# First rows of w_out loaded in halves of columns, five "lower" steps on GpSimd, two products begun ahead of the first transposes

## The chip, the cores and the metric

The kernel runs on one core of a Trainium2 chip. The metric is the device time of one execution in microseconds (us); smaller is better. All inputs are float64 in device memory, so every weight arrives as pairs of 32-bit words and is turned into float32 on the chip.

## What is computed

Causal attention with 12 heads (2 batches, sequence 448, head size 64), then two feed-forward layers on its 896 x 768 output:

```python
scores = scale * q @ k.T                     # causal mask, softmax
x = softmax(scores) @ v                      # 896 x 768
h = ((x @ w1) * (x @ w2)) @ w3 @ w_out       # w1, w2: 768 x 1024, w3: 1024 x 1024, w_out: 1024 x 768
y = relu(h @ w_in2) ** 2 @ w_out2            # w_in2: 768 x 2048, w_out2: 2048 x 768
```

w3 and w_out stand behind each other with nothing between them, so the kernel multiplies w3 @ w_out first, while attention runs, and applies the product W (1024 x 768) later.

## The kernel before, in words

**Attention.** It goes through 12 pairs of heads. A pair p has these steps on TensorE: the scores (`scores`, L611, 16 matmuls, called S below), the transposes of the two heads' probabilities (`transposes`, L684, 20 transposes, T), and the product with v (`attend`, L705, 16 matmuls, A). Between S and T, VectorE takes the masked minimum out of PSUM (L653), ScalarE does the exponential (L663), VectorE takes reciprocals of the sums (L671, L672) and scales the blocks (L680). Between T and A, ScalarE copies the transposes out of PSUM (L701). S and T share six PSUM banks in turn: T of pair 0 reuses those of S of pair 1, so the minimum of pair 1 has to be done before T of pair 0 can end.

**W.** A unit `w_half(g, i, n)` (L549) makes one block of 128 rows by 384 columns (column half n) of W from one row block of w3 and four row blocks of w_out, with g for the two halves of the inner sum; there are 32 units. The first two row blocks of w3 (`PLAIN`, L146) are multiplied in float32 as they are (8 matmuls); the others are split into high and low parts and take 12 matmuls. `w_row` (L506) prepares a whole row block: `load_raw` (L460) issues its load on SP's queue, `float32` (L473) turns the words into float32 in three steps: prelu on ScalarE from the high words (L478), lower on VectorE from the low words, in place (L482), and join on VectorE of both (L486). Where a row is to be split, a cast on ScalarE (L432) and a subtraction on VectorE (L425) follow. Raw rows lie in three buffers taken in turn, and two rows of w_out (`LENT`, L149) in buffers lent by another pool; the second row of w3 comes into the buffer of the first, and so its load waits for the join of the first.

**Order.** The order on TensorE is that in which the steps are added: S0, S1, a filler of 36 transposes of a constant (`warm`, L746), T0, A0, S2, and from there on units of W between the steps (`fill`, L758, and the loop at L762). All other engines get their order from the planner `Program.order` (L59): a step's due time comes from TensorE's order, counted back through the prices given with each step, and at each moment an engine takes the ready step with the earliest due time. A wait written into an engine's queue holds what stands behind it. The weight loads keep their own order among each other (`turn="loads"`, L480).

After attention come w1, w2, W, w_in2 and w_out2, as one stream of matmuls (`bank`).

Of the kernel before, what the change touches and what calls it, by code (L numbers as in the profile page):

```python
# [8 lines left out]
F32 = mybir.dt.float32  # L9
F32R = mybir.dt.float32r  # L10
U32 = mybir.dt.uint32
AF = mybir.ActivationFunctionType
ALU = mybir.AluOpType
# [111 lines left out]
def attention_moe_moe2(ctx: ExitStack, tc: tile.TileContext, qk, v, w1, w2, w3, w_out, w_in2, w_out2, out):  # L125
# [18 lines left out]
    SLOTS8 = 8  # L144
    RAW = 3
    PLAIN = 2  # L146
    WARM = 36
    CLOSE = 4
    LENT = (("wout", 2), ("wout", 3))  # L149
    PAUSE = 64  # L150
# [23 lines left out]
    source = {"wout": w_out, "w1": w1, "w2": w2, "w3": w3, "win2": w_in2, "wout2": w_out2}  # L174
    raws, hls = {}, {}

    def load(key, pool, tag):
        src = source[key[0]][key[1]]
        n = src.shape[-1]
        t = pool.tile([P, DM, 2], U32, tag=tag, name=f"raw_{key[0]}_{key[1]}")  # L180
        nc.sync.dma_start(out=t[:, :n].rearrange("p f w -> p (f w)"), in_=src.bitcast(U32))
        raws[key] = t[:, :n]

    def halves(x):
        return x.rearrange("p (n c) -> p n c", c=HN)
# [147 lines left out]

    prog = Program({"S": 700})
    pools = {}
    engine_of = {"A": nc.scalar, "V": nc.vector}

    def act(width, psum=False, strided=False):
        gap = 60 + 0.815 * width if psum else 75 + (0.96 if strided else 0.845) * width
        return {"A": (gap, gap + 105)}  # L340

    def dve(width, fast=False):
        gap = 70 + (0.52 if fast else 1.038) * width
        return {"V": (gap, gap + 85)}
# [110 lines left out]
    def turn(what, n):  # L455

        count[what] += 1
        return (count[what] - 1) % n

    def load_raw(key):  # L460

        if key in LENT:
            pool, tag, place = ringb, "ringb", ("ringb", turn("lent", 4))
        elif key in order and turn("plain", RAW) == RAW - 1:
            pool, tag, place = rawb, "rawb", ("rawb", 0)
        else:
            pool, tag, place = rawp, "raw", ("raw", turn("raw", 2))
        words = [place + (s,) for s in "hl"]
        size = source[key[0]][key[1]].shape[-1] / DM
        prog.add({"S": (2200 * size, 2500 + 2200 * size)}, lambda e: load(key, pool, tag), [], words, turn="loads")  # L470
        return words

    def float32(key, words, width, y, names):  # L473

        high, low = words

        def prelu(e):
            nc.scalar.activation(y(), raws[key][:, :, 1].bitcast(F32), AF.Prelu, scale=2.0 ** -112, alpha=-2.0 ** 32)  # L478

        def lower(e):  # L480
            x = raws[key][:, :, 0]
            nc.vector.tensor_scalar(x, x, 2.0 ** -29, 7.0, ALU.mult, ALU.min)  # L482

        def join(e):
            yi = y().bitcast(U32)
            nc.vector.scalar_tensor_tensor(  # L486
                yi, yi, 3, raws.pop(key)[:, :, 0], op0=ALU.logical_shift_left, op1=ALU.bitwise_or)

        prog.add(act(width, strided=True), prelu, [high], names)
        prog.add(dve(width, fast=True), lower, [low], [low])  # L490
        prog.add(dve(width), join, [low, *names], names)

# [11 lines left out]
    def w_row(key):  # L506

        if key in w_rows:
            return
        kind, n = key  # L510
        words = load_raw(key)
        if kind == "w3":
            names = [("w3", n % 2, s) for s in "hl"]
            if n < PLAIN:
                w_rows[key] = names[:1]
                float32(key, words, W3N, lambda: w3_tile(n)[:, 0].bitcast(F32), names[:1])
                return
            hi, lo, width = lambda: w3_tile(n)[:, 0], lambda: w3_tile(n)[:, 1], W3N
        elif n < NB:
            names = [("ring", i, s) for i in (2 * n, 2 * n + 1) for s in "hl"]  # L520
            hi, lo, width = lambda: ring_pair(2 * n)[0], lambda: ring_pair(2 * n)[1], DM
        else:
            place = turn("lent", 4)
            names = [("ringb", place, s) for s in "hl"]
            hi, lo, width = lambda: ringb_tile(n)[:, 0], lambda: hls["wout", n][:, 1], DM
        row = 2 + n if kind == "wout" and n < NB else turn("f32", 2)
        x = lambda: xs[:, row, :width]
        src = [("xs", row, i) for i in range(2)]
        float32(key, words, width, x, src)
        y = x if kind == "w3" else lambda: halves(x())  # L530
        his, los = [m for m in names if m[2] == "h"], [m for m in names if m[2] == "l"]
        prog.add(act(width), copy(hi, y), src, his)
        prog.add(dve(width), tt(lo, y, lambda: hi_of(key).bitcast(F32), ALU.subtract), src + his, los)
        w_rows[key] = names

    def hi_of(key):
        kind, n = key
# [11 lines left out]
    def w_half(g, i, n):  # L549
        n3, cols = g * KF + i, slice(n * HN, (n + 1) * HN)  # L550
        plain = n3 < PLAIN
        for key in order[:order.index(("w3", n3)) + 1] + [("wout", g * NB + f) for f in range(NB)]:
            w_row(key)
        place, acc = turn("w", 2), []
        reads = list(w_rows["w3", n3])
        for f in range(NB):
            reads += [("xs", 2 + f, j) for j in range(2)] if plain else w_rows["wout", g * NB + f]

        def run(e):
            acc.append(ps_w.tile([P, HN], F32, tag="w", name=f"w{n3}_{n}"))  # L560
            for f in range(NB):
                c = slice(f * P, (f + 1) * P)
                if plain:
                    mm(acc[0], w3t[n3][:, 0, c].bitcast(F32), xs[:, 2 + f, cols], f == 0, f == NB - 1)
                    continue
                t, wo = w_parts(("w3", n3)), w_parts(("wout", g * NB + f))
                for s, r in ((0, 0), (0, 1), (1, 0)):
                    mm(acc[0], t[s][:, c], wo[r][:, n],
                       f == 0 and (s, r) == (0, 0), f == NB - 1 and (s, r) == (1, 0))

        t0 = (3.72 if plain else 3) * NB * HN * PE_ROW + 100
        prog.add({"T": (t0, t0 + 170)}, run, reads, [("w", place)])
        dst = wraw[i][:, cols]
        if g == 0:
            prog.add(dve(HN) | act(HN, True), copy(lambda: dst, lambda: acc[0]), [("w", place)], [("wraw", i, n)])
            return
        if n == 0:
            add = negated(lambda: dst, lambda: acc[0], lambda: dst, ALU.subtract)
        else:
            add = tt(lambda: dst, lambda: acc[0], lambda: dst, ALU.add)  # L580
        prog.add(dve(HN), add, [("w", place), ("wraw", i, n)], [("wraw", i, n)])
        if n == 1:
            prog.add({"S": (1200, 3000)}, lambda e: nc.sync.dma_start(out=w_dram[i // 2, i % 2], in_=wraw[i]),
                     [("wraw", i, 0), ("wraw", i, 1)], [("wdram", i)])
# [120 lines left out]
    def attend(p):  # L705
        place = turn("w", 2)

        def run(e):
            vt = v_t[p]
            x = x_t[p] = ps_w.tile([P, S], F32, tag="w", name=f"x{p}")  # L710
            for c in range(NCH):
                for j in range(2):
                    mm(x[j * D:(j + 1) * D, c * CP:], vt[:, c, j],
                       pt_t[2 * p + j][:, coff[c]:coff[c] + S - c * CP], c == 0, c == NCH - 1)

        pts = [("pt", h % 3, i) for h in (2 * p, 2 * p + 1) for i in range(len(PT))]
        prog.add({"T": (2038, 2270)}, run, pts + [("v", p % 2)], [("w", place)])
        return place
# [27 lines left out]
    def warm():  # L746
        place = turn("w", 2)

        def run(e):
            t = ps_w.tile([P, HN], F32, tag="w", name="warm")  # L750
            for _ in range(WARM):
                nc.tensor.transpose(t[:CP, :CP], ident[:CP, :CP], ident[:CP, :CP])

        prog.add({"T": (WARM * 96, WARM * 96 + 160)}, run, [], [("w", place)])

    w_units = [(g, i, n) for g in range(N3 // KF) for i in range(KF) for n in range(2)]

    def fill(n=1):  # L758
        for _ in range(n):
            w_half(*w_units.pop(0))  # L760

    for p in range(NP_ALL + 1):  # L762
        if p < NP_ALL:
            load_pair(p)
            load_v(p)
            scores(p)
            for j in range(2):
                softmax(p, j)
        if p == 1:
            warm()  # L770
        if p > 0:
            fill(p > 1)
            transposes(2 * p - 2)
            transposes(2 * p - 1)
            fill(1 if p == NP_ALL else 2 if p >= CLOSE else p > 1)
            place = attend(p - 1)
            x_parts(p - 1, place)
            fill(1 < p < CLOSE)
    assert not w_units

    def end_attention(e):
# [577 lines left out]
```

## Time and profile before

| what | value |
|---|---|
| median of 3 runs | 525.2 us (523.92 to 526.38) |
| the profiled execution's own time | 524.11 us |
| its span | 522.3 us |
| TensorE busy | 511.7 us, 98% of the span |
| VectorE busy | 484.6 us, 93% |
| ScalarE busy | 397.7 us, 76% |
| GpSimd busy | 15.0 us, 3% |

How to read it: the rows further down come from one profiled execution. Times count from the start of the span. PE is TensorE, PEld its weight loads, DVE VectorE, ACT ScalarE, POOL GpSimd, SP the queue that issues most transfers. "L172" is a line of the kernel; where a helper issues all matmuls, the tile's name tells them apart (s: scores, pp: transposes, x: product with v, w: units of W, bank: everything after attention). Brackets behind a row of the timeline hold the idle time ahead of it and what ended it. Float32 matmuls show as two instructions each, so a unit of four float32 products has eight.

### The profile page before, as it was taken

How to read it: one execution, taken by the hardware profiler on the slowest of the kernel's cores; microseconds unless marked ns; L12 is line 12 of the kernel's file. 1: busy time of each engine (PE TensorE's matmuls, PEld its weight loads, DVE VectorE, ACT ScalarE, POOL GpSimd, SP SyncE). 2: the span in 40 equal slices, each digit the busy share in tenths (PEclk: the TensorE clock that was granted, in tenths of full speed). 3: DMA queues.
4: the chain of work that ended last, by engine and by line, in shares of the span. 5: the costliest groups of instructions: out<-in, count | busy, mean ns of one | idle time of the engine just before them, and what ended most of it. 6: DMA issues, size and time to landing. Idle time of an engine off the chain costs nothing.

```text
span 522.3 us, 8468 instructions
## 1 busy us (share of the span) xinstructions
PE 511.7 (98%) x2905; PEld 461.3 (88%) x2905; DVE 484.6 (93%) x1140; ACT 397.7 (76%) x925; POOL 15.0 (3%) x20
## 2 busy tenths in 40 slices
PE   6899999999999999999999999999999999999996
PEld 5658888888889999999999999999999999999996
DVE  5999998889999999988875899999999999999996
ACT  5989988767869574637566568997999689969971
POOL 1000000000000010222100000000000000000000
PEclk9999999999999999999999999999999999999999
DMA  8957455452651459999672311504440355045114
GB/s 318 320 184 227 175 177 169 133 176 63 249 179 65 181 184 248 242 267 259 123 217 95 122 60 44 198 2 148 172 164 1 130 178 177 1 129 184 52 60 152
DMA packets 26571, 81.29 MB, mean 156 GB/s; under 512 B 2400, under 2 KB 13408, under 8 KB 26528
## 3 DMA queue, kind: packets, MB, share of 16 engines
q1 hardware_dynamic: 22752, 75.24, 42.5%
q0 software_dynamic: 3776, 5.51, 6.6%
q8 instruction: 23, 0.38, 0.3%
q14 instruction: 20, 0.16, 0.1%
HBM read 74.84 MB, written 14.55 MB: 171 GB/s over the span
## 4 chain that ended last, share of the span: by engine, by line
PE 94%; ACT 2%; DVE 2%; DMA 1%; issue 0%; DVEq 0%
PE bank L172 69%; PE w L172 13%; PE x L172 4%; PE s L172 4%; PE pp L695 4%; ACT p L663 1%; ACT xs L478 1%; DMA qk<-in_qk 1%; DVE p L653 0%; DVE p L680 0%; ACT pt L701 0%; DVE xs L486 0%; DVE g L425 0%; DVE w L486 0%; ACT w L478 0%; DVE st L672 0%
## 5 line engine op out<-in xcount | busy, mean ns | idle before, releaser
L432 ACT CAST ring<-xs 128x384 fp32r<-128x384 f32 (+1 forms) x194 | 102.7, 545 | 39.7 <-PE bank L172 21.9
L172 PE MATMUL bank<-xT,ring 128*128 128x448 f32 x630 | 132.0, 366 | 0.0
L172 PEld LDWEIGHTS bank<-xT,ring 128*128 128x128 f32 x630 | 117.9, 188 | 9.1
L425 DVE TENSOR_TENSOR ring<-xs,ring 128x384 fp32r<-128x384 f32 (+1 forms) x194 | 111.3, 588 | 13.1 <-ACT ring L432 12.5
L172 PE MATMUL bank<-ring,g 128*128 128x384 f32 x600 | 104.8, 334 | 0.0
L172 PEld LDWEIGHTS bank<-ring,g 128*128 128x128 f32 x600 | 104.1, 188 | 0.2
L172 PE MATMUL bank<-xB,ring 128*128 128x448 f32 x489 | 102.2, 366 | 0.0
L172 PEld LDWEIGHTS bank<-xB,ring 128*128 128x128 f32 x489 | 91.7, 188 | 7.4
L663 ACT ACTIVATE p<-p,st 112x224 f32<-112x224 f32 (+3 forms) x96 | 50.1, 534 | 10.0 <-DVE st L653 10.0
L425 DVE TENSOR_TENSOR xs<-xs 128x384 f32<-128x384 f32 x96 | 51.7, 551 | 0.2
L653 DVE CUSTOM_DVE_ANT_0 p<-s,mask 112x224 f32<-112x224 f32 (+3 forms) x96 | 36.6, 443 | 5.9 <-PE s L172 5.9
L432 ACT CAST g<-fs 128x384 fp32r<-128x384 f32 (+1 forms) x88 | 35.3, 414 | 7.8 <-DVE fs L425 7.7
L425 DVE TENSOR_TENSOR g<-fs,g 128x384 fp32r<-128x384 f32 (+1 forms) x88 | 36.6, 431 | 0.2
L172 PE MATMUL w<-hl_wout,w 128*128 128x384 f32 x192 | 36.2, 340 | 0.0
L432 ACT COPY fs<-bank 128x448 f32<-128x448 f32 (+1 forms) x52 | 27.5, 529 | 8.9 <-PE bank L172 8.7
L172 PEld LDWEIGHTS w<-hl_wout,w 128*128 128x128 f32 x192 | 32.9, 188 | 1.3 <-DVE fs L425 0.9
L172 PE MATMUL s<-qk 64*112 64x112 f32 (+3 forms) x192 | 27.4, 425 | 4.3 <-DMA qk<-in_qk 4.3
L478 ACT ACTIVATE xs<-raw_w 128x768 f32<-128x768 f32 (+1 forms) x30 | 24.2, 812 | 7.0 <-DVE w L425 3.2
L172 PE MATMUL bank<-ab,ring 128*128 128x448 f32 x144 | 29.5, 365 | 0.0
L680 DVE TENSOR_SCALAR p<-p,st 112x448 f32<-112x448 f32 (+1 forms) x96 | 29.1, 360 | 0.1
L172 PEld LDWEIGHTS bank<-ab,ring 128*128 128x128 f32 x144 | 27.1, 188 | 2.1
L172 PEld LDWEIGHTS s<-qk 64*112 64x112 f32 x192 | 15.4, 181 | 14.3 <-issue 6.0
(80 smaller groups left out, 687.2 us busy)
## 6 DMA issues: line engine op xcount, KB each, us to landing
raw_wout<-in_w_out SPq DMA_DIRECT2D x24, 768.0 KB, 4.5
raw_w<-in_w SPq DMA_DIRECT2D x16, 768.0 KB, 4.8
raw_win<-in_w_in SPq DMA_DIRECT2D x16, 768.0 KB, 4.2
raw_w<-in_w SPq DMA_DIRECT2D x16, 512.0 KB, 4.6
qk<-in_qk SPq DMA_DIRECT2D x12, 448.0 KB, 5.3
s_dram<-w_dram POOLq DMA_DIRECT2D x8, 576.0 KB, 9.5
w_dram<-wraw SPq DMA_DIRECT2D x8, 384.0 KB, 2.7
s_dram<-w_dram SPq DMA_DIRECT2D x4, 768.0 KB, 6.9
```

What stands on the lines that cost most here:

```text
L172: return nc.tensor.matmul(o, l, r, start=start, stop=stop, **more)
L425: return lambda e: engine_of[e].tensor_tensor(out(), x(), y(), op=what)
L432: return lambda e: engine_of[e].copy(out(), x()) if e == "A" else engine_of[e].tensor_copy(out(), x())
L478: nc.scalar.activation(y(), raws[key][:, :, 1].bitcast(F32), AF.Prelu, scale=2.0 ** -112, alpha=-2.0 ** 32)
L653: prog.add({"V": (gap, gap + 160)}, lambda e: nc.vector.tensor_tensor_reduce(block(p, j, i), s_t[p, j, g][:CP, o:o + w], mask[:, S - w:], ...
L663: prog.add({"A": (gap, gap + 100)}, lambda e, i=i: nc.scalar.activation(block(p, j, i), block(p, j, i), AF.Exp, bias=st_t[p][:, 0, j, i:i ...
L680: lambda e, i=i: nc.vector.tensor_scalar(block(p, j, i), block(p, j, i), st_t[p][:, 3, j, i:i + 1], None, ALU.mult),
L695: nc.tensor.transpose(x[0][:CP, o * CP:(o + 1) * CP], block(p, j, i)[:, c * CP:(c + 1) * CP], ident[:CP, :CP])
```

## The change

Three things are done.

- The first four row blocks of w_out are loaded and turned into float32 in two halves of 384 columns each, with a step of its own for each half (`w_columns`). A float32 unit of column half n asks for the four halves n only, and for its row of w3.
- The lower step of these eight halves and of the first row of w3 runs on GpSimd (engine "P" of the planner, priced at 100 + 1.3 ns for each column).
- The order on TensorE is written out as a list (`ORDER`; K is the filler, W the next unit). One unit stands between the filler and T0, one between T0 and A0, one each between S2 and T1 and between T1 and A1, and so on; the first four units go by column half: both rows with half 0, then both with half 1. The filler has 20 transposes instead of 36.

```diff
-    WARM = 36
+    WARM = 20
...
-    def load(key, pool, tag):
+    def load(key, pool, tag, cols=None):
         src = source[key[0]][key[1]]
         n = src.shape[-1]
...
+        x, src = raws[key], src.bitcast(U32)
+        if cols is not None:
+            x, src = x[:, cols], src[:, 2 * cols.start:2 * cols.stop]
+        nc.sync.dma_start(out=x.rearrange("p f w -> p (f w)"), in_=src)
...
+    GB, GS = 100, 1.3
+    POOLED = (("w3", 0), *(("wout", f) for f in range(4)))
...
         def lower(e):
-            x = raws[key][:, :, 0]
-            nc.vector.tensor_scalar(x, x, 2.0 ** -29, 7.0, ALU.mult, ALU.min)
+            x = raws[key][:, cols, 0]
+            engine_of[e].tensor_scalar(x, x, 2.0 ** -29, 7.0, ALU.mult, ALU.min)
...
-        prog.add(act(width, strided=True), prelu, [high], names)
-        prog.add(dve(width, fast=True), lower, [low], [low])
-        prog.add(dve(width), join, [low, *names], names)
+        prog.add(act(width, strided=True), prelu, high, names)
+        on_pool = {"P": (GB + GS * width, GB + 100 + GS * width)} if key in POOLED else dve(width, fast=True)
+        prog.add(on_pool, lower, low, low)
+        prog.add(dve(width), join, [*low, *names], names)
...
+    def w_columns(f, c):
+
+        if (f, c) in w_halves:
+            return
+        cols, row = slice(c * HN, (c + 1) * HN), 2 + f
+        w_halves[f, c] = [("xs", row, c)]
+        words = load_raw(("wout", f), cols)
+        float32(("wout", f), words, HN, lambda: xs[:, row, cols], w_halves[f, c], cols)
...
-        for key in order[:order.index(("w3", n3)) + 1] + [("wout", g * NB + f) for f in range(NB)]:
-            w_row(key)
+        if plain:
+            w_row(("w3", n3))
+            for f in range(NB):
+                w_columns(f, n)
+        else:
+            for key in order[:order.index(("w3", n3)) + 1] + [("wout", g * NB + f) for f in range(NB)]:
+                w_row(key)
...
-            reads += [("xs", 2 + f, j) for j in range(2)] if plain else w_rows["wout", g * NB + f]
+            reads += w_halves[f, n] if plain else w_rows["wout", g * NB + f]
...
+    w_units[:4] = [(0, 0, 0), (0, 1, 0), (0, 0, 1), (0, 1, 1)]
...
-    for p in range(NP_ALL + 1):
...
+    ORDER = 'S0 S1 K W T0 W A0 S2 W T1 W A1 S3 W T2 W A2 S4 W T3 W W A3 S5 W T4 W W A4 S6 W T5 W W A5 S7 W T6 W W A6 S8 W T7 W W A7 S9 W T8 W W A8 S10 W T9 W W A9 S11 W T10 W W A10 W T11 W A11'
```

## Rows read from the trace of the kernel before

**Rows 1.** Page, part 1: busy time, share of the span, instructions of each engine.
```profile
PE 511.7 (98%) x2905; PEld 461.3 (88%) x2905; DVE 484.6 (93%) x1140; ACT 397.7 (76%) x925; POOL 15.0 (3%) x20
```

**Rows 2.** Chain that ended last, in time: start us, us, what (pieces on TensorE).
```profile
29.48 2.04 PE x L172 x16
31.52 2.78 PE w L172 x8
34.30 2.08 PE s L172 x16
...
39.16 1.92 PE pp L695 x20
41.07 2.11 PE w L172 x12
...
155.97 360.79 PE bank L172 x1871
```

**Rows 3.** Timeline of TensorE, 0 to 27 us: start, us, instructions, [idle before <-releaser].
```profile
3.94 5.91 PE L172 MATMUL s<-qk 64*112 64x448 f32 x32 [3.94 <-DMA qk<-in_qk]
9.78 3.66 PE L752 MATMUL warm<-ident 112*112 112x112 f32 x36
13.28 2.08 PE L695 MATMUL pp<-ident,p 112*112 112x112 f32 x20
15.29 2.29 PE L172 MATMUL x<-pt,v 112*64 112x448 f32 x16
...
17.90 2.15 PE L172 MATMUL s<-qk 64*112 64x448 f32 x16 [0.33 <-DMA qk<-in_qk]
21.03 2.85 PE L172 MATMUL w<-xs,w 128*128 128x384 f32 x8 [0.98 <-DVE w L486]
...
25.72 1.17 PE L695 MATMUL pp<-ident,p 112*112 112x112 f32 x10 [0.88 <-DVE p L680]
```

**Rows 4.** Busy us of each engine, granted clock, DMA share and GB/s by stretch.
```profile
10.00:15.00 5.00, 5.00 (x54) 5.00 (x53) 4.93 (x27) 5.00 (x14) 0.00 (x0) 1.00 1.01 420
15.00:20.00 5.00, 4.67 (x36) 3.05 (x34) 5.00 (x9) 5.00 (x15) 0.00 (x0) 1.00 1.04 317
```

**Rows 5.** Timeline of SP's queue, 0 to 45 us: issues of the first weight rows.
```profile
2.13 0.42 SPq L181 DMA_DIRECT2D raw_w<-in_w  x1
2.59 2.60 SPq L181 DMA_DIRECT2D raw_wout<-in_w_out  x4
```

**Rows 6.** Loads issued at 2.13, 2.59 and 4.16 us: count, KB, us to landing.
```profile
raw_w<-in_w SPq DMA_DIRECT2D x1, 512.0 KB, 6.2
raw_wout<-in_w_out SPq DMA_DIRECT2D x1, 768.0 KB, 7.6
raw_wout<-in_w_out SPq DMA_DIRECT2D x1, 768.0 KB, 11.8
```

**Rows 7.** Chain that ended last, in time: its pieces on VectorE and ScalarE.
```profile
5.92 0.62 DVE p L653
...
6.59 4.20 ACT p L663 x16
10.79 0.83 ACT xs L478
11.62 0.59 ACT w L478
...
20.38 0.60 DVE w L486
```

**Rows 8.** Timeline of VectorE, 10 to 35 us.
```profile
14.60 1.50 DVE L482 TENSOR_SCALAR raw_wout<-raw_wout 128x768 uint32<-128x768 uint32 x3
...
17.68 2.69 DVE L486 SCALAR_TENSOR_TENSOR xs<-xs,raw_wout 128x768 uint32<-128x768 uint32 x3
...
33.18 1.18 DVE L680 TENSOR_SCALAR p<-p,st 112x448 f32<-112x448 f32 x4
```

**Rows 9.** Timeline of GpSimd, 0 to 45 us: its last instruction there.
```profile
1.64 0.55 POOL L328 TENSOR_SCALAR_AFFINE_SELECT mask<-mask 112x448 f32<-112x448 f32 x1
```

More of the change, by code (lines that the diff above doesn't have):

```diff
@@ L175, in attention_moe_moe2 @@
     raws, hls = {}, {}
-    def load(key, pool, tag):
+    def load(key, pool, tag, cols=None):
         src = source[key[0]][key[1]]
         n = src.shape[-1]
-        t = pool.tile([P, DM, 2], U32, tag=tag, name=f"raw_{key[0]}_{key[1]}")
-        nc.sync.dma_start(out=t[:, :n].rearrange("p f w -> p (f w)"), in_=src.bitcast(U32))
-        raws[key] = t[:, :n]
+        if key not in raws:
+            t = pool.tile([P, DM, 2], U32, tag=tag, name=f"raw_{key[0]}_{key[1]}")
+            raws[key] = t[:, :n]
+        x, src = raws[key], src.bitcast(U32)
+        if cols is not None:
+            x, src = x[:, cols], src[:, 2 * cols.start:2 * cols.stop]
+        nc.sync.dma_start(out=x.rearrange("p f w -> p (f w)"), in_=src)
     def halves(x):
@@ L335, in attention_moe_moe2 @@
     pools = {}
-    engine_of = {"A": nc.scalar, "V": nc.vector}
+    engine_of = {"A": nc.scalar, "V": nc.vector, "P": nc.gpsimd}
+    GB, GS = 100, 1.3
+    POOLED = (("w3", 0), *(("wout", f) for f in range(4)))
     def act(width, psum=False, strided=False):
@@ L458, in turn, with load_raw, float32 @@
         return (count[what] - 1) % n
-    def load_raw(key):
-        if key in LENT:
-            pool, tag, place = ringb, "ringb", ("ringb", turn("lent", 4))
+    def load_raw(key, cols=None):
+        if cols is not None and key in raw_place:
+            place = raw_place[key]
+        elif key in LENT:
+            place = ("ringb", turn("lent", 4))
         elif key in order and turn("plain", RAW) == RAW - 1:
-            pool, tag, place = rawb, "rawb", ("rawb", 0)
+            place = ("rawb", 0)
         else:
[L467 to L473, printed above, removed]
+            place = ("raw", turn("raw", 2))
+        width = source[key[0]][key[1]].shape[-1]
+        if cols is not None:
+            raw_place[key] = place
+            words = [place + (s, cols.start // HN) for s in "hl"]
+            width = cols.stop - cols.start
+        else:
+            words = [place + (s, c) for s in "hl" for c in range(2)]
+        size = width / DM
+        pool, tag = {"raw": (rawp, "raw"), "rawb": (rawb, "rawb"), "ringb": (ringb, "ringb")}[place[0]]
+        prog.add({"S": (2200 * size, 2500 + 2200 * size)}, lambda e: load(key, pool, tag, cols), [], words, turn="loads")
+        return words[:len(words) // 2], words[len(words) // 2:]
+    raw_place = {}
+    def float32(key, words, width, y, names, cols=slice(None)):
         high, low = words
         def prelu(e):
-            nc.scalar.activation(y(), raws[key][:, :, 1].bitcast(F32), AF.Prelu, scale=2.0 ** -112, alpha=-2.0 ** 32)
+            nc.scalar.activation(y(), raws[key][:, cols, 1].bitcast(F32), AF.Prelu, scale=2.0 ** -112, alpha=-2.0 ** 32)
         def lower(e):
-            x = raws[key][:, :, 0]
-            nc.vector.tensor_scalar(x, x, 2.0 ** -29, 7.0, ALU.mult, ALU.min)
+            x = raws[key][:, cols, 0]
+            engine_of[e].tensor_scalar(x, x, 2.0 ** -29, 7.0, ALU.mult, ALU.min)
         def join(e):
@@ L486, in join @@
             nc.vector.scalar_tensor_tensor(
-                yi, yi, 3, raws.pop(key)[:, :, 0], op0=ALU.logical_shift_left, op1=ALU.bitwise_or)
-        prog.add(act(width, strided=True), prelu, [high], names)
-        prog.add(dve(width, fast=True), lower, [low], [low])
-        prog.add(dve(width), join, [low, *names], names)
+                yi, yi, 3, raws[key][:, cols, 0], op0=ALU.logical_shift_left, op1=ALU.bitwise_or)
+        prog.add(act(width, strided=True), prelu, high, names)
+        on_pool = {"P": (GB + GS * width, GB + 100 + GS * width)} if key in POOLED else dve(width, fast=True)
+        prog.add(on_pool, lower, low, low)
+        prog.add(dve(width), join, [*low, *names], names)
     w3t, w_rows = {}, {}
@@ L510, in w_row @@
         kind, n = key
-        words = load_raw(key)
+        if kind == "wout" and n < NB:
+            for c in range(2):
+                w_columns(n, c)
+        else:
+            words = load_raw(key)
         if kind == "w3":
@@ L528, in w_row @@
         src = [("xs", row, i) for i in range(2)]
-        float32(key, words, width, x, src)
+        if kind == "w3" or n >= NB:
+            float32(key, words, width, x, src)
         y = x if kind == "w3" else lambda: halves(x())
@@ L534, in w_row @@
         w_rows[key] = names
+    def w_columns(f, c):
[5 more added lines that the diff above has]
+        float32(("wout", f), words, HN, lambda: xs[:, row, cols], w_halves[f, c], cols)
+    w_halves = {}
     def hi_of(key):
@@ L551, in w_half @@
         plain = n3 < PLAIN
-        for key in order[:order.index(("w3", n3)) + 1] + [("wout", g * NB + f) for f in range(NB)]:
-            w_row(key)
+        if plain:
+            w_row(("w3", n3))
+            for f in range(NB):
+                w_columns(f, n)
+        else:
+            for key in order[:order.index(("w3", n3)) + 1] + [("wout", g * NB + f) for f in range(NB)]:
+                w_row(key)
         place, acc = turn("w", 2), []
@@ L760, in fill @@
             w_half(*w_units.pop(0))
-    for p in range(NP_ALL + 1):
-        if p < NP_ALL:
+    ORDER = 'S0 S1 K W T0 W A0 S2 W T1 W A1 S3 W T2 W A2 S4 W T3 W W A3 S5 W T4 W W A4 S6 W T5 W W A5 S7 W T6 W W A6 S8 W T7 W W A7 S9 W T8 W W A8 S10 W T9 W W A9 S11 W T10 W W A10 W T11 W A11'
+    for step in ORDER.split():
+        p = int(step[1:] or 0)
+        if step[0] == "W":
+            fill()
+        elif step[0] == "K":
+            warm()
+        elif step[0] == "S":
             load_pair(p)
@@ L768, in attention_moe_moe2 @@
                 softmax(p, j)
[L769 to L778, printed above, removed]
+        elif step[0] == "T":
+            transposes(2 * p)
+            transposes(2 * p + 1)
+        else:
+            x_parts(p, attend(p))
     assert not w_units
```

## The prediction

> **What bounds the kernel now.** I read the page first, then the chain that ended last, then the waits of TensorE, and only then the other engines where those waits point. TensorE is busy for 98% of the span [rows 1], and from 25.72 us on the chain consists of TensorE's pieces alone, up to the 360.79 us stream of matmuls that ends the kernel [rows 2]. The timeline of TensorE carries no wait behind that at 25.72 us [rows 3]. So the end is fixed by the moment at which TensorE gets out of the first 26 us, plus a sum that the change leaves as it is but for 16 transposes of the filler.
>
> In those 26 us TensorE stands still four times: 3.94 us until the first scores' input has landed, 0.33 us for the third pair's input, 0.98 us for the join of w3's first row, 0.88 us for pair 1's scaled blocks [rows 3]. Behind the last two is VectorE, busy 4.93 and 5.00 of 5 us between 10 and 20 us, with ScalarE at 5.00 and the transfers at full share too [rows 4]. The filler (3.50 us from 9.78 to 13.28) is no work either: it fills the time in which VectorE gets ready for T0.
>
> **The size of the prize.** I compare the time at which one and the same set of steps is done: S0 to S3, T0 to T2, A0, A1, the filler, four float32 units and the first split unit. Before, that is 41.07 + 2.11 = 43.18 us [rows 2]. Without any wait the steps behind the filler take 4 x 2.78 (units) + 3 x 1.92 (T) + 2 x 2.04 (A) + 2 x 2.08 (S) + 2.2 (split unit, a little above its 2.11) = 27.3 us [rows 2]. With the filler, 9.78 + 3.50 + 27.3 = 40.6, so the waits there cost 2.6 us. The shorter filler gives 16/36 x 3.50 = 1.56 us and ends at 11.72. The most there is to gain is 2.6 + 1.56 = 4.2 us; what is kept of it depends on when the first unit can start.
>
> **Loading in halves.** w3's row was issued at 2.13 and landed 6.2 us later, at 8.3; w_out's rows, issued within 2.60 us from 2.59 on [rows 5], landed from 2.59 + 7.6 = 10.2 to 4.16 + 11.8 = 16.0 us [rows 6]. Three more rows took 5.8 us, 1.93 us a row, 0.97 us a half. The halves of one column, placed behind w3's row, land by 8.3 + 4 x 0.97 = 12.2 us, or by 11.6 if v of pair 0 falls behind them, as its later due time lets the planner do (224 KB, 0.56 us at this rate). I take 11.9. Four more issues of 0.42 us on SP [rows 5] cost nothing so early, since the transfers are the limit.
>
> **The first unit.** From the last landing it needs a prelu, a lower beside it, and a join. The prelu of 768 columns takes 0.83 us and of 512 columns 0.59 [rows 7], so 384 take 0.47. The join takes 2.69 / 3 = 0.90 us for 768 [rows 8] and 0.60 for 512 [rows 7], so 0.45 for 384. The lower on GpSimd has no row: the only nearby one is an operation of 448 columns on 112 partitions at 0.55 us [rows 9], so about 0.5 us is its lower end; upwards no row binds it. I take the planner's 0.60 us (0.77 for w3's row), because its prices for the three steps on the other engines (0.81, 0.47, 0.87 us for 768 columns) lie within some 6% of the rows (0.83, 0.50, 0.90). The Trainium skill, GPSIMD Engine Reference, Performance pitfalls for Q7 kernels, gives about 1.9 cycles an element for reads up to 8 bytes apart, which at its 1.2 GHz would be an estimate of 0.61 us; no row here shows it, and the sum would be the same. So the unit starts at 11.9 + 0.60 + 0.45 + some 0.1 of hand-over = 13.0 us, 1.3 us behind the end of the filler.
>
> **VectorE up to T0.** Before, all that S0, S1 and the scaling of pair 0 need ran from 5.92 [rows 7] to 14.60 us without a gap, 8.68 us [rows 8]. Now the joins of w3's row and of four halves come in between, 0.60 + 4 x 0.45 = 2.4 us, so VectorE is through at 17.0. TensorE begins T0 at 13.0 + 2.78 = 15.8 and works bank by bank, to 17.7; only its last bank can be late. The second unit needs w3's second row: a lower and a join on VectorE, 0.33 + 0.60, so 17.9 and some hand-over. For these two I put 0.6 us of waiting. What is cheaper: the lowers of 4 rows (0.50 each) and of w3's row (0.33) leave VectorE, 2.3 us; 4 more joins add 4 x (2 x 0.45 - 0.90), about nothing, up to 0.3 us with the fixed part of an instruction. ScalarE's prelus go from 4 x 0.83 to 8 x 0.47, 0.4 us more; it has 4.20 us of exponentials of pair 0 [rows 7] and 2.5 us of the first prelus from 6.59 on, so it is through at 13.3, in time for T0.
>
> **Waits that the change adds.** On SP, the load of w3's second row waits until the join of the first has freed its buffer, now at some 9 to 10 us instead of 20.98; v of pair 0, the third pair's input and the second halves stand behind it. All of them together land by about the time at which the third pair's input came before (just short of 17.9), the second halves some 2 us later, and the steps that use them come at 20.9 (A0), 22.9 (S2) and 25.0 us (third unit). That hides it; if the join slipped by over 5 us, A0 and S2 would be late. On GpSimd nothing else is queued. On TensorE the unit ahead of T0 holds T0, the scores of pair 2 and all behind them.
>
> **The sum.** 13.0 + 27.3 + 0.6 = 40.9 us against 43.18: 2.3 us earlier. Later stages keep it: before, the scaling of pair 2 was done at 33.18 + 1.18 = 34.4 [rows 8] for a T2 at 39.16 [rows 2], 4.8 us ahead, and VectorE now has 2 us less to do. The profiled execution would go from 524.11 to 521.8, the median from 525.2 to **522.9 us**.
>
> **Rivals.**
>
> *All ready when the filler ends (0.15).* If loads and joins are 1.3 us quicker than I think and T0 finds its blocks, the whole 4.2 us are kept: 521.0. For it: the halves are small and the second unit fills the time in which ScalarE copies T0's results. Against it: transfers at full share up to 20 us [rows 4].
>
> *GpSimd and VectorE hold each other up (0.22).* Nothing in this trace has GpSimd compute while VectorE works; its last instruction in these stages is at 1.64 us [rows 9]. If a lower keeps VectorE's joins and scalings out while it runs, the five lowers take up to 4 x 0.60 + 0.77 = 3.2 us out of the engine that is the limit up to the second unit; the loss is anything from 0 to 3.2 us, the result 522.9 to 526.1, and half of it, 524.5, is what I would put. The Trainium skill, SBUF — State Buffer, Who interferes with whom, speaks for this: a VectorE instruction with two SBUF inputs, or in a mode that uses both ports, and a GpSimd instruction that reads SBUF exclude each other for a whole instruction, and the first to start blocks the other. The joins have two SBUF inputs; no row of before shows the effect. Against it: most of VectorE's work up to 10 us is the minimum, which reads PSUM and one SBUF tensor.
>
> *GpSimd is slow (0.11), the case on the other side.* The five lowers run one after the other from about 7.4 us on, and the first unit waits for the last of them, with T0 and all else behind it. With 2.5 us each the last is done at 19.9, the unit starts at 20.4, and 20.4 + 27.3 = 47.7: 4.5 us late, 529.7 us. It decides from the point at which the unit starts later than 43.18 - 27.3 = 15.9 us, that is, from 1.6 us a lower, 2.7 times the planner's price. For it: no row bounds the price from above. Against it: the 0.55 us [rows 9].
>
> *The lead is given back (0.05).* A new order by the planner may make another stage late, and the time stays 525.2. Against it: 4.8 us of slack at T2.
>
> **How the numbers follow.** The forecast, 522.9, has 0.47; its own range is 521.9 to 524.0 (0.3 us each for landing, waits, and units of 2.60 instead of 2.78 us behind T, and the scatter of the runs). About 0.5% (2.6 us, below 522.6 or above 527.8) is what a measurement of this kernel can tell from no change. Faster by that: the first rival and 0.4 of the forecast, 0.34. Slower: the slow GpSimd, 0.11. Within: the rest, 0.55. The range goes from 520.8 to 526.1: it takes in the whole prize and the full blocking, and leaves the slow GpSimd out.
>
> **What would show it.** In the changed profile I look for: the first unit's matmuls at about 13.0 us, released by a join (L486 before); a lower on GpSimd of about 0.6 us; T0 at 15.8; the second unit near 18; the first split unit and T2 both done at about 40.9 instead of 43.18; and no wait of TensorE behind that. Wrong would be: lowers over 1.6 us, joins or scalings on VectorE longer than before while GpSimd works, the first unit waiting for a transfer at 13 us or later, or new waits of TensorE behind 41 us.

## The result: slower, 1.0% where 0.4% less was forecast

The changed kernel takes 530.56 us (median), the kernel before 525.55 in the same runs: ratio 1.0102, 95% interval 1.0086 to 1.0118. The forecast was 522.9 us, with a range of 520.8 to 526.1. The profiled execution has a span of 528.0 us against 522.3.

The page of the changed kernel, its busy times and the clock granted to TensorE in 40 slices, answers to [rows 1]:

```profile
PE 514.8 (98%) x2889; PEld 460.9 (87%) x2889; DVE 484.9 (92%) x1139; ACT 398.6 (75%) x929; POOL 31.9 (6%) x29
...
PEclk9799999999999999999999999999999999999999
```

GpSimd has nine instructions (five rows, four of them in two halves) and 16.9 us more, and the second slice (13 to 26 us) shows a lower clock, which no slice of before does. Pieces of the chain that ended last, changed kernel (answers to [rows 2]):

```profile
44.52 2.31 PE w L172 x12
46.82 1.92 PE pp L734 x20
...
162.00 361.07 PE bank L172 x1871
```

The set of steps that the prediction compares is done at 46.82 + 1.92 = 48.74 us; before it was at 43.18, forecast 40.9. The long stream starts at 162.00 us instead of 155.97, 6.0 us later, and is as long as it was. So 5.6 us of the loss are in the head. Behind it TensorE has no long wait; another 0.5 us goes near 120 us, where a T takes 2.45 us instead of 2.08 and the unit behind it starts late. Timeline of TensorE, changed kernel (answers to [rows 3]):

```profile
9.72 2.13 PE L791 MATMUL warm<-ident 112*112 112x112 f32 x20
11.99 0.91 PE L172 MATMUL w<-xs,w 128*128 128x384 f32 x2
13.99 0.91 PE L172 MATMUL w<-xs,w 128*128 128x384 f32 x2 [1.09 <-DVE xs L503]
15.97 0.91 PE L172 MATMUL w<-xs,w 128*128 128x384 f32 x2 [1.07 <-DVE xs L503]
17.97 1.65 PE L172 MATMUL w<-xs,w 128*128 128x384 f32 x2 [1.08 <-DVE xs L503]
19.41 1.91 PE L734 MATMUL pp<-ident,p 112*112 112x112 f32 x10
22.45 1.00 PE L734 MATMUL pp<-ident,p 112*112 112x112 f32 x7 [1.13 <-DVE p L719]
24.21 0.64 PE L734 MATMUL pp<-ident,p 112*112 112x112 f32 x3 [0.76 <-DVE st L692]
24.64 4.35 PE L172 MATMUL w<-xs,w 128*128 128x384 f32 x8
```

The first unit comes in four pieces 2 us apart, each released by a join (L503). T0 ends at 24.8 us instead of 15.3, and the second unit takes 4.35 us where 2.8 are usual. What the joins wait for stands in the timelines of GpSimd and of VectorE, changed kernel (GpSimd answers to [rows 9], VectorE to [rows 8]):

```profile
7.17 2.01 POOL L499 TENSOR_SCALAR raw_w<-raw_w 128x512 uint32<-128x512 uint32 x1 [4.97 <-DMA raw_w<-in_w]
9.26 15.17 POOL L499 TENSOR_SCALAR raw_wout<-raw_wout 128x384 uint32<-128x384 uint32 x8
```

```profile
11.37 0.56 DVE L503 SCALAR_TENSOR_TENSOR xs<-xs,raw_wout 128x384 uint32<-128x384 uint32 x1 [1.46 <-POOL raw_wout L499]
...
13.38 0.56 DVE L503 SCALAR_TENSOR_TENSOR xs<-xs,raw_wout 128x384 uint32<-128x384 uint32 x1 [0.90 <-POOL raw_wout L499]
...
15.36 0.56 DVE L503 SCALAR_TENSOR_TENSOR xs<-xs,raw_wout 128x384 uint32<-128x384 uint32 x1 [0.29 <-POOL raw_wout L499]
15.83 0.73 DVE L719 TENSOR_SCALAR p<-p,st 112x448 f32<-112x448 f32 x1
...
17.35 0.56 DVE L503 SCALAR_TENSOR_TENSOR xs<-xs,raw_wout 128x384 uint32<-128x384 uint32 x1 [0.79 <-POOL raw_wout L499]
```

Eight lowers of 384 columns take 15.17 us, 1.9 us each, and follow each other from 9.26 to 24.43 us. VectorE, which had no idle time here before, waits for each of them in the order of its queue, while the minimum and scaling that T0 needs stand behind the waiting join. Lastly the clock, in stretches of the changed kernel (columns as in [rows 4]; the value ahead of the last two is the granted clock):

```profile
17.00:19.00 2.00, 1.03 (x2) 0.53 (x3) 1.65 (x5) 0.00 (x0) 1.92 (x2) 0.65 1.06 379
19.00:21.00 2.00, 2.00 (x10) 1.73 (x10) 1.97 (x8) 1.02 (x3) 1.92 (x2) 0.50 1.02 353
25.00:27.00 2.00, 2.00 (x4) 1.01 (x4) 0.78 (x3) 2.00 (x6) 0.00 (x0) 0.50 0.74 242
```

Behind the pieces with waits of 1.1 us between them TensorE runs at half its clock (1.2 instead of 2.4 GHz), and again behind T0's waits; the second unit falls into that.

### The profile page after: what moved, and what is told of

Its sections match the earlier page's. It is cut to its first block, busy times and chain, and to the rows that moved or that the text cites. A ratio compares the mean times of both kernels' runs of the same rounds, so it can differ in the third digit from the quotient of the medians.

```text
span 528.0 us, 8463 instructions
## 1 busy us (share of the span) xinstructions
PE 514.8 (98%) x2889; PEld 460.9 (87%) x2889; DVE 484.9 (92%) x1139; ACT 398.6 (75%) x929; POOL 31.9 (6%) x29
## 3 DMA queue, kind: packets, MB, share of 16 engines
q1 hardware_dynamic: 23328, 75.24, 42.2%
## 4 chain that ended last, share of the span: by engine, by line
PE 88%; DVE 5%; DMA 2%; POOL 2%; ACT 2%; issue 0%; SPq 0%; ACTq 0%
PE bank L172 68%; PE w L172 10%; PE x L172 3%; PE pp L734 3%; PE s L172 3%; DMA raw_w<-in_w 2%; POOL raw_wout L499 1%; DVE p L719 1%; ACT p L702 1%; DVE p L692 1%; DVE xs L503 1%; DVE fs L431 0%; ACT pt L740 0%; POOL raw_w L499 0%; DVE g L431 0%; DVE w L431 0%
## 5 line engine op out<-in xcount | busy, mean ns | idle before, releaser
L719 DVE TENSOR_SCALAR p<-p,st 112x448 f32<-112x448 f32 (+1 forms) x96 | 30.3, 371 | 0.1
L740 ACT COPY pt<-pp 112x448 f32<-112x448 f32 (+1 forms) x72 | 28.0, 476 | 0.9 <-PE pp L734 0.9
```

The source lines that it names most:

```text
L719: lambda e, i=i: nc.vector.tensor_scalar(block(p, j, i), block(p, j, i), st_t[p][:, 3, j, i:i + 1], None, ALU.mult),
L740: prog.add(act(width, True), lambda e, gi=gi, x=x, width=width: nc.scalar.copy(pt_t[h][:, coff[PT[gi][0]]:coff[PT[gi][0]] + width], x[0][: ...
```

## The experiments

The question was whether the price of a lower on GpSimd accounts for the whole miss, or whether the new order, the halves or the clock have a share. "Set done" is the end of the compared set of steps (43.18 us before); a ratio is against the kernel before on the same chip, with its 95% interval.

| run | time, us | ratio | set done at, us |
|---|---|---|---|
| changed kernel | 530.56 | 1.0102 (1.0086 to 1.0118) | 48.74 |
| e1, lowers on VectorE | 526.38 | 1.0012 (0.9997 to 1.0027) | 43.08 |
| e2, GpSimd alone | 530.87 | 1.0098 (1.0066 to 1.0130) | 50.22 |
| e3, filler of 84 | 532.43 | 1.0125 (1.0102 to 1.0148) | 50.05 |
| e5, true price | 526.80 | 1.0016 (1.0001 to 1.0031) | 45.97 |
| e6, lowers left out | 523.99 | 0.9965 (0.9947 to 0.9984) | 41.66 |
| e7, halves alone | 524.75 | 0.9995 (0.9985 to 1.0006) | 42.27 |
| e8, halves, old units | 524.53 | 0.9995 (0.9985 to 1.0004) | 43.33 |
| e9, a unit behind A0 | 525.65 | 1.0004 (0.9991 to 1.0017) | 42.2 |
| e10, seven of nine on GpSimd | 525.53 | 1.0002 (0.9984 to 1.0020) | 44.64 |
| e11, as e9 with GpSimd | 527.29 | 1.0045 (1.0026 to 1.0064) | 44.0 |
| e12, filler of 20 alone | 524.35 | 0.9979 (0.9970 to 0.9988) | 43.31 |

The kernel before took 525.6 us beside e1, e2, e3 and e5, 524.95 beside e6 to e8 and 525.2 beside e9 to e12. "Set done" comes from the one profiled execution of each run, and its own time can lie off the median: 525.11 us in e1, 532.11 in e2, 522.28 in e6, 526.66 in e10.

**What a lower costs on GpSimd (e4).**

```diff
+    def price(x, a=2.0 ** -29, b=7.0):
+        nc.gpsimd.tensor_scalar(x, x, a, b, ALU.mult, ALU.min)
...
+    price(pairs(xu, 384))
+    price(pairs(xu, 512))
+    price(pairs(xu, 768))
+    price(xu[:, :384])
+    price(pairs(xf, 384))
+    price(xf[:, :384])
```

Here `xu` is a tile as uint32 and `xf` as float32; `pairs` takes every second word, as the lower does.

> The kernel before with seven extra GpSimd instructions at the start, on a tile that is not in use yet: a memset, then the lower's two operations (multiply, minimum) on uint32 with every second word for 384, 512 and 768 columns, on 384 adjacent uint32, and on 384 float32 with every second word and adjacent. If the stride sets the price, the adjacent forms are faster by a third or more; if the uint32 arithmetic does, the float32 forms are; if it is the number of elements alone, all forms of 384 take the same, 1.5 us undisturbed, and 768 takes 2.9 to 3.1 us. If VectorE and GpSimd hold each other up, those that run beside VectorE's joins and scalings (behind 10 us) are 0.3 to 0.5 us longer than the same form earlier, and VectorE's scalings of 448 columns take more than their 0.45 us.

Groups of GpSimd's instructions by shape, this run (busy us, mean ns of one):

```profile
L339 POOL TENSOR_SCALAR xs<-xs 128x384 uint32<-128x384 uint32 x2 | 3.1, 1560 | 0.2
L339 POOL TENSOR_SCALAR xs<-xs 128x384 f32<-128x384 f32 x2 | 3.1, 1558 | 0.2
L339 POOL TENSOR_SCALAR xs<-xs 128x768 uint32<-128x768 uint32 x1 | 2.9, 2921 | 0.1
L339 POOL TENSOR_SCALAR xs<-xs 128x512 uint32<-128x512 uint32 x1 | 2.0, 2002 | 0.1
```

The number of elements alone sets the price: 1.56 us for 384 columns, (2921 - 1560) / 384 = 3.5 ns for each further column, whatever type or stride. That is 2.6 times the 0.60 us of the forecast. The four forms of 384 columns lie between 1.51 and 1.60 us, those that ran beside VectorE's scalings too; it was the scalings that grew (timeline of VectorE, this run, against 1.18 us for four before [rows 8]):

```profile
10.79 1.83 DVE L697 TENSOR_SCALAR p<-p,st 112x448 f32<-112x448 f32 x4
```

So GpSimd does hold VectorE up, by some 0.16 us a scaling here. The one execution took 525.33 us.

**GpSimd alone (e2).** The five lowers on GpSimd in the kernel before, whole rows and old order:

```diff
+    POOLED = (("w3", 0), *(("wout", f) for f in range(4)))
...
-            nc.vector.tensor_scalar(x, x, 2.0 ** -29, 7.0, ALU.mult, ALU.min)
+            engine_of[e].tensor_scalar(x, x, 2.0 ** -29, 7.0, ALU.mult, ALU.min)
...
```

> The kernel before with only the five lowers put on GpSimd (whole rows, old order, filler of 36). Theory 1: at 1.9 us for 384 columns a row of 768 takes 3 to 3.9 us, the last lower ends at 23 to 26 us, the first unit starts 3 to 5 us later than at 21.03, and the time is 528 to 531 us. Rival (the order costs, not GpSimd): 524 to 526 us.

Timelines of GpSimd and of VectorE (pair 0's eight scalings), this run:

```profile
9.47 2.17 POOL L484 TENSOR_SCALAR raw_w<-raw_w 128x512 uint32<-128x512 uint32 x1 [7.26 <-DMA raw_w<-in_w]
11.72 13.55 POOL L484 TENSOR_SCALAR raw_wout<-raw_wout 128x768 uint32<-128x768 uint32 x4
```

```profile
10.67 2.27 DVE L683 TENSOR_SCALAR p<-p,st 112x448 f32<-112x448 f32 x4
13.55 2.45 DVE L683 TENSOR_SCALAR p<-p,st 112x448 f32<-112x448 f32 x4
```

The lowers end at 25.3 us, and the time is that of the changed kernel. This part alone, without the halves and the new order, makes a loss of the same size. It does so in part by another way: T0 needs no lower, but pair 0's scalings took 2.27 + 2.45 us beside GpSimd's instructions instead of 1.19 + 1.19, and the second half of T0 begins only at 16.06 us. T0 ends 2.2 us later than before for that reason alone: GpSimd held VectorE up, and no join that waits for a lower has a part in it.

**The rest without GpSimd (e1).** In the changed kernel all lowers go back to VectorE:

```diff
-    POOLED = (("w3", 0), *(("wout", f) for f in range(4)))
+    POOLED = ()
```

> The changed kernel with all lower steps back on VectorE; halves, list of steps and the filler of 20 stay. Theory 1, the GpSimd lowers alone cost the time: the first unit starts near 13.3 us, T0 ends near 18.6, the second unit starts near 19.3, T2 and the first split unit are done near 42 us instead of 48.74, and the time is 523.5 to 524.5 us, below the kernel before. Rival, the new order itself costs (a unit ahead of T0 makes T0 late whatever engine does the lowers): at least half of the loss stays, 527 us or more.

Timeline of TensorE, and its only wait behind 60 us, this run:

```profile
12.35 2.76 PE L172 MATMUL w<-xs,w 128*128 128x384 f32 x8
16.09 1.19 PE L734 MATMUL pp<-ident,p 112*112 112x112 f32 x10 [0.98 <-DVE p L719]
18.65 1.00 PE L734 MATMUL pp<-ident,p 112*112 112x112 f32 x7 [1.37 <-DVE p L719]
20.26 0.50 PE L734 MATMUL pp<-ident,p 112*112 112x112 f32 x3 [0.61 <-DVE st L692]
```

```profile
PE w L172 <- DVE w L431: 0.7, 1, 0.7
```

The first unit starts at 12.35 us, earlier than I expected, and the loss is gone. But no gain comes: T0 waits 3.0 us for VectorE, and the set is done only 0.1 us earlier than before. The time is 0.8 us above that of before, within its interval, where 1 to 2 us below were expected. Part of that is given back later: the long stream starts at 156.95 us, 1.0 us later than before, behind a wait at 82 us. Pieces of this run's chain ahead of that wait:

```profile
69.64 3.90 DMA raw_w<-in_w
...
74.29 2.42 ACT p L702 x8
...
82.05 2.01 PE w L172 x10
```

A load of a w3 row, then ScalarE's exponentials and copies, then a join and a subtraction come too late for that unit in the planner's new order.

**The lowers for nothing (e6).** The nine lowers are left out, and the join takes the low words as they are, with an and in place of the or. The product is then wrong altogether, not only in its lowest bits; the run is for the time alone:

```diff
+        if key not in POOLED:
             prog.add(on_pool, lower, low, low)
...
-                yi, yi, 3, raws[key][:, cols, 0], op0=ALU.logical_shift_left, op1=ALU.bitwise_or)
+                yi, yi, 3, raws[key][:, cols, 0], op0=ALU.logical_shift_left,
+                op1=ALU.bitwise_and if key in POOLED else ALU.bitwise_or)
```

> The changed kernel with the nine GpSimd lowers (w3's first row and the eight halves) left out altogether, so that part of the float64 words is not used (the join takes an and in place of an or, the same instruction otherwise). It gives the lowers the price zero and leaves every other term of the forecast. Theory 1 (only the price of the lower was wrong): the first unit starts at 12.5 to 13.5 us, T0 ends at 17.5 to 18.5, T2 and the first split unit are done at 40.5 to 41.5 us, and the time is 522.5 to 524 us. Rival (the forecast's sum for VectorE up to T0 was too low as well): T0 ends later than 19 us and the time is 524.5 us or more.

Timeline of TensorE, and two pieces of the chain, this run:

```profile
11.92 2.76 PE L172 MATMUL w<-xs,w 128*128 128x384 f32 x8
14.66 1.20 PE L736 MATMUL pp<-ident,p 112*112 112x112 f32 x10
17.22 1.00 PE L736 MATMUL pp<-ident,p 112*112 112x112 f32 x7 [1.36 <-DVE p L721]
18.84 0.50 PE L736 MATMUL pp<-ident,p 112*112 112x112 f32 x3 [0.61 <-DVE st L694]
```

```profile
17.98 0.60 DVE w L503
18.59 0.18 DVE p L694
...
39.74 1.92 PE pp L736 x20
...
154.22 319.76 PE bank L172 x1648
```

The set is done at 39.74 + 1.92 = 41.66 us, 0.8 later than the 40.9 forecast, and the 1.5 us of lead stay to the end (the long stream starts 1.75 us earlier, the span is 520.5). T0 ends at 19.3 instead of 17.7 us. It waits 1.36 us for pair 0's scalings, which VectorE has done at 17.0 us only, and 0.61 us for the last minimum of pair 1, which stands in VectorE's queue behind the join of w3's second row. The second unit is then 1.0 us later than in my sum; two units of 2.60 us behind a T, where I had put 2.78, give a part of it back. Each expectation is met by half: T0 ends later than 19 us, as the rival had it, but the time, 523.99 us, lies in the range of theory 1.

**The planner told the truth (e5).** The lowers stay on GpSimd; only their price in the planner is 1.93 us:

```diff
-    GB, GS = 100, 1.3
+    GB, GS = 1930, 0.0
```

> The changed kernel with the planner's price of a GpSimd lower set to 1.93 us, as measured, instead of 0.60 and 0.77. The lowers stay on GpSimd; only the order changes. If VectorE's queue is held up by joins that stand ahead of work that T0 needs (VectorE was busy only 6.6 of 10 us between 10 and 20 us), the planner now puts minimum and scaling first, T0 comes right behind the first unit, and the time falls by 2 to 4 us, to 526.5 to 528.5. If only the unit's own wait counts, it stays within 1 us of 530.6.

Timeline of TensorE, a stretch (columns as in [rows 4]) and the end of T2 in the chain, this run:

```profile
16.31 0.91 PE L172 MATMUL w<-xs,w 128*128 128x384 f32 x2 [1.37 <-DVE xs L503]
18.88 0.91 PE L172 MATMUL w<-xs,w 128*128 128x384 f32 x2 [1.66 <-DVE xs L503]
19.62 2.08 PE L734 MATMUL pp<-ident,p 112*112 112x112 f32 x20
21.54 2.76 PE L172 MATMUL w<-xs,w 128*128 128x384 f32 x8
```

```profile
17.00:19.00 2.00, 0.34 (x2) 0.13 (x2) 2.00 (x9) 1.22 (x6) 1.92 (x2) 1.00 1.05 374
```

```profile
45.47 0.50 PE pp L734 x3
```

The first unit is as late as in the changed kernel, but VectorE works through its waits, T0 follows without one, the clock stays at 1.00 in this execution, and 2.8 us of the head, 3.8 us of the time, are gone. So that much of the miss is the order that the planner made from a wrong price, with the clock that fell behind it, and not the price itself. The order of the loads moved too, so that GpSimd begins at 6.24 us instead of 7.17; up to 0.9 us of the gain may be due to that and not to VectorE's queue.

**A filler that keeps TensorE busy (e3).**

```diff
-    WARM = 20
+    WARM = 84
```

> The changed kernel with a filler of 84 transposes instead of 20, which keeps TensorE busy until about 17.9 us, when the last half is joined. If the lower clock (0.50 from 17.6 to 21.0 and from 24.6 to 27.5 us) is a large part of the loss, the clock stays at 1.00, the units ahead of A0 take 2.8 us each instead of up to 4.35, and the time falls by 1.5 to 3 us, to 527.5 to 529 us. If the clock is a small part, T0 and the units are still set by VectorE and the time stays within 0.7 us of 530.6.

Timeline of TensorE and a stretch, this run:

```profile
17.96 2.76 PE L172 MATMUL w<-xs,w 128*128 128x384 f32 x8
...
25.21 2.76 PE L172 MATMUL w<-xs,w 128*128 128x384 f32 x8
28.57 2.75 PE L172 MATMUL x<-pt,v 112*64 112x448 f32 x16 [0.60 <-ACT pt L740]
```

```profile
19.00:21.00 2.00, 2.00 (x11) 1.28 (x10) 1.97 (x10) 0.34 (x1) 1.92 (x2) 1.00 0.79 256
```

The clock stays at 1.00 and the second unit takes 2.76 us again, 1.6 less. Nothing is won: the first unit starts only when the filler is through and ends 1.1 us later than in the changed kernel, T0 waits for VectorE as before and ends 0.5 us later (GpSimd began at 7.75 us, 0.6 later), and A0 then waits for ScalarE. Neither expectation fits, the run is slower by some 1.9 us. Other waits took the clock's place, so this run does not give its share.

The single executions say more about that share. In e10 (below) seven with a mean granted clock of 0.998 or more took 524.39 to 525.55 us, five with 0.995 to 0.997 took 526.16 to 528.04; the profiled one is of the latter, and the unit behind its T0 takes 4.45 us. In e2 two at 1.000 and 0.997 took 529.15 and 529.63 us, two at 0.993 and 0.992 took 532.11 and 533.05. All six of the changed kernel lie at 0.989 to 0.992, while executions of the kernel before do not differ so (524.5 to 528.2 us at 0.997, 524.4 to 528.2 at 1.000). An estimate from these, if nothing else sets the two groups apart: the lower clock is worth some 1.6 us in e10 and 3 us in e2. In e5 and e6 such groups overlap, and what the clock is worth in the changed kernel is not shown.

**Parts and other orders (e7 to e12).** The halves alone, lowers on VectorE, filler and steps as before (e8 with the units in the old sequence as well). The edit is that of e1 and:

```diff
-    WARM = 20
+    WARM = 36
-    ORDER = 'S0 S1 K W T0 W A0 S2 W T1 W A1 S3 ...
+    ORDER = 'S0 S1 K T0 A0 S2 W T1 W A1 W S3 ...
```

> The halves of w_out's rows and the order of the first four units by column half, but the steps on TensorE, the filler of 36 and the lowers on VectorE as before. The first unit needs half of the joins and lowers, so it should follow S2 without the wait of 0.98 us, at about 20.1 us, and T1 should find pair 1's scaling done: 1 to 1.9 us less, 523.7 to 524.7 us. If the load of w3's second row, which waits for the first row's join and holds the second halves and the third pair's input back, is what counts, S2 or the second unit is late and the time is 526 us or more.

> As the run with halves alone, but with the first four units in the old sequence, both halves of w3's first row and then both of the second. The second unit then needs the second halves near 23 to 26 us and no early second row of w3. If a late second row of w3 is a hindrance, this one is faster than the run with halves alone, by up to 1 us; if VectorE's sum is all that counts, they agree within 0.5 us, at 523.7 to 524.7 us.

In e7 the first unit follows S2 without a wait, at 19.77 us, as expected, but T1 still waits 0.9 us for VectorE; the set is done 0.9 us earlier. Neither run can be told from the kernel before, and they agree within 0.3 us. With one unit between A0 and S2 (e9), and the same with all nine lowers on GpSimd at the true price (e11); the edit is shown against e7:

```diff
-    ORDER = 'S0 S1 K T0 A0 S2 W T1 W A1 W S3 W T2 W A2 W S4 ...
+    ORDER = 'S0 S1 K T0 A0 W S2 W T1 W A1 W S3 W T2 W A2 S4 ...
```

> Halves with all lowers on VectorE and the filler of 36, and one unit (of the first halves) placed between A0 and S2, not ahead of T0. The theory is that VectorE's sum up to T0 sets the head, so that a unit's joins belong behind T0's work: T0 stays near 13.3 us, A0 ends near 17.6, the first unit starts near 18.4 with a wait of 0.8 us, and T2 and the first split unit are done near 41.5 instead of 43.18 us: 523.3 to 524.3 us, the best so far with all lowers done. Rival (every order ends at the same sum of VectorE's work): within 0.5 us of the kernel before.

> As the run with one unit between A0 and S2, but with the nine lowers on GpSimd at the true price of 1.93 us. Four lowers of first halves and w3's end near 17 us, ahead of the unit at 18.4, so they are off the path, and VectorE has 2.5 us less to do. If that relief counts, the time is 0.5 to 1.5 us below the run with VectorE's lowers; if GpSimd and VectorE hold each other up by as much (VectorE's scalings went from 1.19 to 1.83 us for four beside GpSimd's instructions), it is the same or up to 1 us slower.

e9 has its first unit at 18.43 us, as expected, and the set done at 42.2, 1.0 us ahead of before; its long stream starts at 156.49, 0.5 us later than before, behind waits of 1.0 us near 80 us like that of e1. Here the lead is given back, and the time, 0.45 us above that of before, is what the rival had expected. e11 is slower than e9: VectorE's relief brings nothing. Its first two units come when those of e9 do, but then the third waits 0.42 us for a join and the fourth 0.80 us for a copy, both on VectorE. Why VectorE is late with these is not shown. In the changed kernel, at the true price, with two lowers of first halves on VectorE (e10):

```diff
-    GB, GS = 100, 1.3
+    GB, GS = 1930, 0.0
...
-... if key in POOLED else dve(width, fast=True)
+... if key in POOLED and not (cols.start == 0 and key[1] > 1) else dve(width, fast=True)
```

> The changed kernel with the price of a GpSimd lower at 1.93 us in the planner and two of the four first halves' lowers on VectorE, so that GpSimd has three lowers ahead of the first unit and not five. If the chain of lowers on GpSimd sets the first unit (7.2 us + 2.0 + n x 1.9), the unit starts near 13.5 us instead of 19, and the time falls below the 526.8 us of the run with the true price alone, to 524.5 to 525.5 us. If VectorE's sum takes over, T0 ends at 19 to 20 us and the time is 525.5 to 526.8 us.

The unit starts at 12.45 us, but T0 waits 2.0 us for VectorE and ends at 20.6: 525.53 us, as expected if VectorE's sum takes over, and the same as before. Last, the kernel before with the short filler:

```diff
-    WARM = 36
+    WARM = 20
```

> The kernel before with a filler of 20 transposes instead of 36 and nothing else. T0 is set by VectorE (its work for T0 ends at 14.60 us), so T0 ends where it did, the 1.56 us turn into waits, and the time stays within 0.7 us of the kernel before. If the filler were in T0's way, 1 to 1.5 us would be gained.

The waits take the place of the filler (T0 0.62 us, the first unit 1.68 instead of 0.98) and the set is done at 43.31 us, as before. The time is 0.2% lower all the same; nothing in the head of this trace shows why, and that stays open.

## Why the prediction was wrong, step by step

- **TensorE alone sets the end, and the head decides: right.** The set was 5.6 us late, the span 5.7 us longer, with no wait of note behind 24.64 us.
- **Landings: right.** The halves came early enough for the first unit to start at 11.92 us in e6 and 12.35 in e1, against 13.0 (in e1 the last of them landed at 11.44, forecast 11.9); the transfers' waits that the change adds on SP (v, third pair, second halves) held up nothing.
- **The price of a lower on GpSimd: this step failed.** I took 0.60 us because the planner's prices fitted the rows of other engines. Those fits say nothing of an engine without a row. Alone it is 1.56 us for 384 columns (e4), and 1.9 to 2.1 for the five that began within 0.05 us of a join in the changed kernel. So the fifth lower ended at 17.33 us, and the first unit, forecast to run from 13.0 to 15.8, was done at 19.6. The estimate of 0.61 us from the Trainium skill, GPSIMD Engine Reference, Performance pitfalls for Q7 kernels, agreed with the wrong price; at the 1.2 GHz given there the measured 3.5 ns a column are 4.3 cycles and not 1.9, and the stride makes no difference.
- **What follows from that price: only half named.** My rival of the slow GpSimd turns at 1.6 us a lower, and 1.9 us lie beyond. The 1.56 us of a lower alone do not: by the rival's sum (7.4 + 2.0 + 4 x 1.56 + 0.5 + 27.3 = 43.4) they would about keep the old time (43.18). By this estimate the loss needs the holding up, or the planner's order, as well as the price. With the lowers as measured the fourth half's ends just ahead of its join at 17.35 us, the whole unit could start at 17.9, and 17.9 + 27.3 = 45.2: 2.0 us late, 527.6. Measured are 5 us. What it missed is VectorE's order: joins planned for 0.60 us stood ahead of T0's minimum and scaling and kept them waiting. e5 takes this away and comes out at 526.8. Of the 7.8 us between the forecast 40.9 and 48.74, 2.8 go with the wrong order (48.74 to 45.97, the clock among it), 4.3 with GpSimd's real price and its hold on VectorE (45.97 to 41.66, e6), and 0.8 with my own sum.
- **VectorE up to T0: mis-sized.** With lowers at no price T0 and the second unit still waited 2.0 us, not 0.6: the sum of VectorE's work came out 0.7 us low (done with the second w3 join at 18.6, forecast 17.9). That only T0's last bank could be late was wrong: the scalings, too, were done only at 17.0, and the join stood ahead of the last minimum.
- **GpSimd and VectorE hold each other up: real, and not small in sum.** My rival had 0 to 3.2 us for it. In the changed kernel a scaling of 448 columns took 0.73 us instead of 0.45, and pair 0's eight scalings 1.1 us more in all; the four lowers behind w3's took 7.8 us instead of 4 x 1.56 = 6.2. In e2 the scalings alone took 2.3 us more. How much of the 4.3 us above is this and how much is GpSimd's own price stays open.
- **The lead stays: right for e6, not for every order.** It also stayed in e7's trace (0.9 us), though its time does not show it. e1, e9, e10 and e11 lost 1.1 to 1.5 us between the set and the long stream, e1 and e9 with waits near 80 us. The 4.8 us of slack that I read at T2 do not hold for each later unit.
- **The chances.** A price without a row above got a 0.11 for its slow side, though I had no row against it but one of another operation. The range should have reached over it.

## What to carry to other kernels

A price that no row shows has to be measured before a bottleneck is moved onto it, and a planner's figure is no row, however well its other figures fit; until then the forecast's range has to take in several times that price. It has to be measured beside the work that will run next to it: the lower took 1.56 us alone and 1.9 to 2.1 right behind the start of a join, and VectorE's scalings grew beside it as well. In a kernel whose queues are laid out by prices, a price that is too low costs twice: the step is late, and everything that the planner put behind it on another engine waits with it. Where the engine that frees the bottleneck is itself full, earlier placement of a unit only changes which step waits for it.

## What the runs showed of the hardware

- An elementwise operation on GpSimd with two scalar operands takes 1.56 us for 384 columns and 2.92 for 768, the same for uint32 and float32, with adjacent words or every second one (e4: 1.51 to 1.60 us for 384); VectorE's took 0.36 us (e1) and 0.56 (before).
- The Trainium skill, SBUF — State Buffer, Who interferes with whom, lets the later of a VectorE and a GpSimd instruction that contend for their shared ports wait for the whole of the first; a VectorE instruction with at most one SBUF input, outside the modes with two ports, does not contend. In part the traces agree: VectorE's minimum, with PSUM and one SBUF input, kept its 0.62 us, and a join that began just ahead of a lower (11.37 against 11.42 us) kept its 0.56 while the lower grew to 1.93. But a scaling that began 0.4 us into a lower of 1.93 us was done 0.73 us later, with 0.8 us of the lower still to run; it lost 0.28 us, not the rest of the lower.
- The granted clock fell to 0.50 behind waits of 1.1 us (changed kernel, 17.6 us), but stayed at 1.00 in e5's profile with waits of 1.4 and 1.7 us and TensorE busy for only 0.34 of the 2 us from 17 to 19. What makes the difference no run here shows.
